# The last row tile of an attention and feed-forward kernel, computed and stored in three column pieces instead of two

## The chip, the cores and the metric

The kernel runs on one core of one Trainium2 chip. The metric is the device time of one execution in microseconds (us); a time is given as the median of several runs.

## What is computed

The reference has two parts. The first is a linear attention with a decay for each head, in blocks of 64 positions with a state that is carried from block to block. The second takes the attention's output as 3,072 rows of 512 and sends it through a feed-forward layer with a sine in it. Cut to what matters:

```python
# attention: q, k, v of (4, 8, 768, 64), lam of (8,)
for b in range(12):                                    # blocks of 64 positions
    intra = (qb @ kb^T * Dmask) @ vb                   # within the block
    inter = (qb * lam_pow) @ kv_state                  # from the blocks before
    out[block] = intra + inter
    kv_state = lam**64 * kv_state + (kb * rev_pow)^T @ vb

# feed-forward: x of (3072, 512), w_in of (512, 2048), w_out of (2048, 512)
h = x @ w_in
s = np.sin(alpha * h)
g = h + s * s / (alpha + 1e-09)
result = g @ w_out                                     # (3072, 512) float32
```

## The kernel before

The rows are treated in six groups of 512, each as four row tiles of 128. A long list, `ORDER`, gives the order in which every step is handed to its engine; a step is written `name.indices:engine:bank`, with T for TensorE, V for VectorE, A for ScalarE, G for GpSimd and S for SyncE. At its end stands group 5. The second product of a row tile is `f2` (sixteen matmuls into one bank of PSUM), its copy to SBUF is `oc`, and its store is `st`, once for each half of the partitions. The last row tile, the fourth of group 5, has steps of its own: `lt` for the matmuls and `ltc` for copy and store.

```python
# the end of ORDER
f2.5.1.0:T:2 f2.5.1.1:T f2.5.1.2:T f2.5.1.3:T f2.5.2.0:T:5 f2.5.2.1:T f2.5.2.2:T oc.5.1:V f2.5.2.3:T
st.5.1.0:S st.5.1.1:S lt.0:T:3 oc.5.2:V st.5.2.0:S lt.1:T:7 st.5.2.1:S ltc.0:A ltc.1:A
...
BANK = ("h0", "h1", "h2", "h3", "s0", "s1", "oa", "ob")

def psum(shape, dtype, name, bank):
    bank = bank[0] if isinstance(bank, list) else bank
    return ps.tile(shape, dtype, name=name, tag=BANK[bank], bufs=1)
...
outp = ctx.enter_context(tc.tile_pool(name="outp", bufs=4))
...
def copy(eng, out, in_):
    if eng is nc.scalar:
        nc.scalar.copy(out=out, in_=in_)                # line 281
    else:
        eng.tensor_copy(out=out, in_=in_)               # line 283
...
def ffn2(g, m, j, bank, **_):
    ...
        nc.tensor.matmul(out=ops[g, m][:], lhsT=gall[g][:, f, m * P:(m + 1) * P],   # line 524
                         rhs=w_out_sb[:, f, :], start=(f == 0), stop=(f == NFC - 1))

def store(g, m, par, **_):                              # line 539
    nc.sync.dma_start(out=out_rows(g, m)[par], in_=obs[g, m][par * D:(par + 1) * D, :])

last = {}

def last_tile(i, bank, **_):
    h = DM // 2                                         # 256 columns
    last[i] = psum([P, h], FP32, "ops", bank)
    for f in range(NFC):                                # 16 matmuls, line 547
        nc.tensor.matmul(out=last[i][:], lhsT=gall[NG - 1][:, f, 3 * P:],
                         rhs=w_out_sb[:, f, i * h:(i + 1) * h],
                         start=(f == 0), stop=(f == NFC - 1))

def last_copy(i, eng, **_):
    h = DM // 2
    rows = out_rows(NG - 1, 3)
    ob = outp.tile([P, h], FP32, name="ob")
    copy(eng, ob[:], last[i][:])
    for par, queue in ((0, nc.sync), (1, nc.scalar if i else nc.sync)):   # stores, line 557
        queue.dma_start(out=rows[par][:, i * h:(i + 1) * h], in_=ob[par * D:(par + 1) * D, :])
```

Two other steps have instructions of the form that the change brings in, 128 columns on the whole array or 128 columns from PSUM: `interm` (line 445), which multiplies the queries by the carried state, and `kv_copy`, which copies the key-value product (tile `kva`) out of PSUM with `copy`. Line 326 turns a 128 by 128 block with a matmul against the identity. Line 618 is the program's end, where all engines meet and SyncE waits for every store.

Of the kernel before, what the change touches and what calls it, by code (L numbers as in the profile page):

```python
# [11 lines left out]
FP32 = mybir.dt.float32  # L12
# [110 lines left out]
f2.4.2.3:T f2.4.3.0:T:0 f2.4.3.1:T f2.4.3.2:T f2.4.3.3:T f2.5.0.0:T:3 f2.5.0.1:T f2.5.0.2:T oc.4.2:V  # L123
oc.4.3:A st.4.3.0:S st.4.2.0:S st.4.3.1:S st.4.2.1:S f2.5.0.3:T oc.5.0:V st.5.0.0:S st.5.0.1:S
f2.5.1.0:T:2 f2.5.1.1:T f2.5.1.2:T f2.5.1.3:T f2.5.2.0:T:5 f2.5.2.1:T f2.5.2.2:T oc.5.1:V f2.5.2.3:T
st.5.1.0:S st.5.1.1:S lt.0:T:3 oc.5.2:V st.5.2.0:S lt.1:T:7 st.5.2.1:S ltc.0:A ltc.1:A
"""

@with_exitstack
def kernel(  # L130
# [12 lines left out]
    P = nc.NUM_PARTITIONS  # L143

    B, H, S, D = q.shape
# [5 lines left out]
    DM, DFF = moe_w_in.shape  # L151
# [17 lines left out]
    outp = ctx.enter_context(tc.tile_pool(name="outp", bufs=4))  # L169
# [29 lines left out]
    for c in range(2):  # L199
# [14 lines left out]
        out=mask[:], in0=it.rearrange("p two e -> p (two e)").unsqueeze(1)  # L214
# [20 lines left out]
    w_out_sb = wpool.tile([P, NFC, DM], BF16, name="w_out_sb")  # L235
# [5 lines left out]
# [3 lines that stand above are left out]
# [35 lines left out]
    def copy(eng, out, in_):  # L279
        if eng is nc.scalar:  # L280
            nc.scalar.copy(out=out, in_=in_)  # L281
        else:
            eng.tensor_copy(out=out, in_=in_)  # L283
# [193 lines left out]
    ops = {}  # L477
# [51 lines left out]
    def out_rows(g, m):  # L529
        _, tp, b, _, _ = where(4 * g + 2 * (m // 2))  # L530
        r0 = b * S + tp * W + (m % 2) * C
        return out[r0:r0 + C].rearrange("(p two) d -> two p d", two=2)
# [7 lines left out]

    last = {}

    def last_tile(i, bank, **_):
        h = DM // 2
        last[i] = psum([P, h], FP32, "ops", bank)
        for f in range(NFC):
            nc.tensor.matmul(out=last[i][:], lhsT=gall[NG - 1][:, f, 3 * P:],  # L547
                             rhs=w_out_sb[:, f, i * h:(i + 1) * h],
                             start=(f == 0), stop=(f == NFC - 1))

    def last_copy(i, eng, **_):
        h = DM // 2
        rows = out_rows(NG - 1, 3)
        ob = outp.tile([P, h], FP32, name="ob")
        copy(eng, ob[:], last[i][:])
        for par, queue in ((0, nc.sync), (1, nc.scalar if i else nc.sync)):
            queue.dma_start(out=rows[par][:, i * h:(i + 1) * h], in_=ob[par * D:(par + 1) * D, :])

    bz = ps.tile([P, 2 * P], FP32, name="bz", tag="h1", bufs=1)
    for _ in range(N0):  # L560
# [9 lines left out]
    def alphas(**_):  # L570
# [7 lines left out]
          "s": scores, "m": domask, "k": kvmm, "kc": kv_copy, "ap": alpha_turn, "al": alphas, "a": kv_decayed, "n": kv_next,  # L578
          "oi": interm, "o": outmm, "x": outev, "f1a": ffn1_first, "f1": ffn1, "sin": sine, "sqr": square,
          "stt": snake, "f2": ffn2, "oc": out_copy, "st": store, "lt": last_tile,  # L580
          "ltc": last_copy}
    def warm_up(n, tag):
# [40 lines left out]
```

## Time and profile before

| | before |
|---|---|
| time, median of 3 runs | 217.11 us (216.66 to 217.22) |
| span of the profiled run | 214.7 us |
| TensorE busy | 206.3 us, 96% of the span |
| last row tile: 32 matmuls of 128x256 | from 207.12 us, 3.66 us |
| copies of its two pieces on ScalarE | at 209.06 and 210.81 us, 0.37 us each |
| last two stores | issued at 211.21 us, one on SyncE and one on ScalarE |

Times inside a run count from the start of the profiled span. On the page, PE is TensorE's matmul side, PEld its weight loads, DVE VectorE, ACT ScalarE, POOL GpSimd and SP SyncE; a q behind an engine means its instruction queue, where the issue of a DMA is shown. A row of digits divides the span into 40 equal slices of 5.4 us, with the busy share of each in tenths. A group of instructions is given as line, engine, operation, the tiles written and read, the shapes, a count, the busy time and the mean length of one in ns; after the second bar stands how long the engine was idle before them and what ended that. A line of the timeline is start, length, engine, line, operation and count, with the idle time before it in brackets.

### The profile page before, as it was taken

The page shows a single profiled execution, that of the slowest core. Times are in us where ns is not written, and L with a number is a line of the kernel's source. Part 1 is how long each engine was busy: PE and PEld are TensorE (multiplying, and loading weights), DVE is VectorE, ACT ScalarE, POOL GpSimd, SP SyncE. Part 2 cuts the span into 40 slices and gives each one's busy share as a digit, 9 for nine tenths or more (in the row PEclk, how much of TensorE's full clock was granted, in tenths as well). Part 3 has the DMA queues.
Part 4 walks back from the last instruction along what each step waited for, and adds up shares of the span by engine and source line. Part 5 has one row for each costly group of instructions (what it writes and reads, how often), then busy time and mean ns, then how long its engine had stood idle before and what let it go on. Part 6 is the DMA issues. An engine that isn't in the chain of part 4 may idle for free.

```text
span 214.7 us, 5454 instructions
## 1 busy us (share of the span) xinstructions
PE 206.3 (96%) x2116; PEld 109.7 (51%) x2116; DVE 129.6 (60%) x234; ACT 123.8 (58%) x244; POOL 141.5 (66%) x208
## 2 busy tenths in 40 slices
PE   7999999897999999999998999999999999999992
PEld 5667544455744554455544554454454444444462
DVE  3894897157599854778756785726884635441120
ACT  2564993075899849996494496936635659131000
POOL 5496399699497999999998986709841738030000
PEclk9999999999999999999999999999999999999998
DMA  5999999999999999969799799720610000171624
GB/s 137 296 238 198 204 202 264 288 294 266 165 190 213 247 226 277 243 120 196 212 257 119 180 194 231 93 49 0 135 41 3 0 0 0 43 166 38 148 53 94
DMA packets 63849, 33.92 MB, mean 158 GB/s; under 512 B 19648, under 2 KB 60880, under 8 KB 63824
## 3 DMA queue, kind: packets, MB, share of 16 engines
q1 hardware_dynamic: 59488, 29.31, 62.6%
q0 software_dynamic: 4224, 4.19, 12.2%
q8 instruction: 16, 0.26, 0.6%
q10 hardware_dynamic: 112, 0.07, 0.1%
q14 instruction: 9, 0.07, 0.1%
HBM read 27.28 MB, written 6.29 MB: 156 GB/s over the span
## 4 chain that ended last, share of the span: by engine, by line
PE 72%; DMA 11%; POOL 4%; SPq 4%; ACT 4%; issue 2%; DVE 1%; POOLq 0%; ACTq 0%
PE ops L524 31%; PE hps L481 30%; DMA w_out_sb<-in_moe_w_out_dram 4%; SPq L258 4%; DMA st_v<-in_v_dram 3%; DMA QT<-KD 3%; PE sp L367 2%; PE okv L459 2%; ACT s L501 2%; DMA st_k<-in_k_dram 2%; PE ops L547 2%; PE okv L445 2%; POOL KD L299 1%; PE kvp L399 1%; POOL QL L299 1%
## 5 line engine op out<-in xcount | busy, mean ns | idle before, releaser
L481 PE MATMUL hps<-xt,w_in_sb 128*128 128x512 bf16 (+1 forms) x416 | 87.5, 363 | 0.0
L524 PE MATMUL ops<-w_out_sb,gall 128*128 128x512 bf16 x368 | 85.9, 379 | 0.6 <-DMA w_out_sb<-in_moe_w_out_dram 0.6
L515 DVE SCALAR_TENSOR_TENSOR gall<-s,r_sb,hps 128x512 bf16<-128x512 bf16 x96 | 68.3, 743 | 23.6 <-POOL s L510 12.0
L501 ACT ACTIVATE s<-hps,alpha_sb 128x512 bf16<-128x512 f32 x96 | 63.2, 689 | 25.8 <-PE hps L481 25.1
L510 POOL TENSOR_TENSOR s<-s 128x512 bf16<-128x512 bf16 x35 | 36.4, 1048 | 37.8 <-ACT s L501 37.1
L481 PEld LDWEIGHTS <-w_in_sb 128*128 128x128 bf16 x416 | 39.7, 98 | 40.7
L524 PEld LDWEIGHTS <-gall 128*128 128x128 bf16 x368 | 34.6, 98 | 40.2 <-issue 0.9
L377 DVE TENSOR_TENSOR ST<-sp,mask 128x512 bf16<-128x512 f32 x48 | 31.8, 684 | 4.4 <-PE sp L367 4.2
L508 ACT ACTIVATE s<-s 128x512 bf16<-128x512 bf16 x51 | 31.6, 633 | 1.0 <-DVE gall L515 0.4
L299 POOL TENSOR_TENSOR QL<-st_q,E 128x512 bf16<-128x512 f32 x23 | 24.0, 1045 | 3.7 <-DVE KD L299 2.1
L283 DVE COPY ob<-ops 128x512 f32<-128x512 f32 x12 | 8.3, 690 | 26.7 <-PE ops L524 23.4
L299 POOL TENSOR_TENSOR KD<-st_k,R 128x512 bf16<-128x512 f32 x22 | 22.9, 1045 | 2.0 <-DMA st_k<-in_k_dram 2.0
L424 POOL TENSOR_TENSOR kvbd<-kvx,LBD 128x256 bf16<-128x256 f32 x32 | 19.6, 614 | 2.5
L281 ACT COPY ob<-ops 128x512 f32<-128x512 f32 (+1 forms) x13 | 7.2, 555 | 23.3 <-PE ops L547 12.9
L281 ACT CAST xt<-okv 128x256 bf16<-128x256 f32 x29 | 9.8, 374 | 12.6 <-PE okv L459 12.4
L420 POOL TENSOR_TENSOR kvx<-kva,kvs 128x128 f32<-128x128 f32 x32 | 14.8, 463 | 1.4 <-ACT kva L281 1.2
L283 DVE CAST xt<-okv 128x256 bf16<-128x256 f32 x19 | 7.7, 419 | 11.0 <-PE okv L459 11.0
L281 ACT COPY kva<-kvp 128x128 f32<-128x128 f32 x26 | 6.4, 273 | 9.2 <-PE kvp L399 8.2
L281 ACT COPY QT<-pt 128x512 bf16<-128x512 bf16 x9 | 5.2, 585 | 10.1 <-PE pt L326 10.1
L367 PE MATMUL sp<-QT 64*64 64x128 bf16 x384 | 9.9, 219 | 0.9 <-DMA QT<-KD 0.9
L459 PE MATMUL okv<-ST,VB 64*64 64x128 bf16 x384 | 9.9, 220 | 0.0
L281 ACT CAST VB<-st_v 128x512 bf16<-128x512 f32 x14 | 8.6, 622 | 1.6 <-DMA st_v<-in_v_dram 1.6
(57 smaller groups left out, 126.9 us busy)
## 6 DMA issues: line engine op xcount, KB each, us to landing
st_q<-in_q_dram SPq DMA_DIRECT2D x24, 256.0 KB, 4.8
st_k<-in_k_dram SPq DMA_DIRECT2D x24, 256.0 KB, 4.7
st_v<-in_v_dram SPq DMA_DIRECT2D x24, 256.0 KB, 5.6
out_dram<-ob SPq DMA_DIRECT2D x46, 128.0 KB, 2.8
w_in_sb<-in_moe_w_in_dram POOLq DMA_DIRECT2D x4, 512.0 KB, 7.8
w_out_sb<-in_moe_w_out_dram POOLq DMA_DIRECT2D x4, 512.0 KB, 11.9
QT<-QL SPq DMA_TRANSPOSE x16, 3.2
QT<-KD SPq DMA_TRANSPOSE x16, 3.8
```

Of the source, the lines that this page charges most:

```text
L281: nc.scalar.copy(out=out, in_=in_)
L283: eng.tensor_copy(out=out, in_=in_)
L299: eng.tensor_tensor(out=t[:], in0=stage[u, j][:].rearrange("p h two e -> p two h e"), in1=tab[:, :, hh * HH:(hh + 1) * HH].unsqueeze(3).to ...
L377: nc.vector.tensor_tensor(out=stm[u][:, hd], in0=sps[u][hd][:], in1=mask[:].unsqueeze(2).to_broadcast([P, 2, 2, P]), op=ALU.mult)
L420: eng.tensor_tensor(out=t[:], in0=x, in1=prev[:], op=ALU.add)
L424: eng.tensor_tensor(out=kvbd[u, c][:], in0=x.unsqueeze(2).to_broadcast([P, 2, 2, D]), in1=LBD[:, 2 * hh:2 * hh + 2, :].unsqueeze(3).to_bro ...
L481: f1mm[g, f] = nc.tensor.matmul(out=hps[g, f][:].rearrange("p (b i) -> p b i", b=2)[:, bs] .rearrange("p b i -> p (b i)"), lhsT=w_in_sb[:, ...
L501: nc.scalar.activation(out=s1[g, f][:], in_=hps[g, f][:], func=ACTF.Sin, scale=alpha_sb[:, f:f + 1])
L508: nc.scalar.activation(out=s2[g, f][:], in_=x[:], func=ACTF.Square)
L510: eng.tensor_tensor(out=s2[g, f][:], in0=x[:], in1=x[:], op=ALU.mult)
L515: nc.vector.scalar_tensor_tensor(out=gall[g][:, f, :], in0=s2.pop((g, f))[:], scalar=r_sb[:, f:f + 1], in1=hps.pop((g, f))[:], op0=ALU.mul ...
L524: nc.tensor.matmul(out=ops[g, m][:], lhsT=gall[g][:, f, m * P:(m + 1) * P], rhs=w_out_sb[:, f, :], start=(f == 0), stop=(f == NFC - 1))
```

## The change

The last row tile is computed in three pieces of 256, 128 and 128 columns instead of two of 256. The first two are copied by ScalarE and the third by VectorE, so that the piece that ends last is smaller, and its copy is on an engine of its own. As before, the first piece is stored from SyncE's queue alone, and each later piece half from SyncE's and half from ScalarE's. The purpose is to shorten what is left to do once TensorE has finished. The number of multiplications and the bytes stored stay the same; there are 48 matmuls instead of 32 in this tile, three copies instead of two, and six stores instead of four.

```diff
-st.5.1.0:S st.5.1.1:S lt.0:T:3 oc.5.2:V st.5.2.0:S lt.1:T:7 st.5.2.1:S ltc.0:A ltc.1:A
+st.5.1.0:S st.5.1.1:S lt.0:T:3 oc.5.2:V st.5.2.0:S lt.1:T:7 st.5.2.1:S ltc.0:A lt.2:T:5 ltc.1:A
+ltc.2:V
...
+    LAST = ((0, 256), (256, 128), (384, 128))
+
     def last_tile(i, bank, **_):
-        h = DM // 2
-        last[i] = psum([P, h], FP32, "ops", bank)
+        c0, n = LAST[i]
+        last[i] = psum([P, n], FP32, "ops", bank)
         for f in range(NFC):
             nc.tensor.matmul(out=last[i][:], lhsT=gall[NG - 1][:, f, 3 * P:],
-                             rhs=w_out_sb[:, f, i * h:(i + 1) * h],
+                             rhs=w_out_sb[:, f, c0:c0 + n],
                              start=(f == 0), stop=(f == NFC - 1))
 
     def last_copy(i, eng, **_):
-        h = DM // 2
+        c0, n = LAST[i]
         rows = out_rows(NG - 1, 3)
-        ob = outp.tile([P, h], FP32, name="ob")
+        ob = outp.tile([P, n], FP32, name="ob")
         copy(eng, ob[:], last[i][:])
         for par, queue in ((0, nc.sync), (1, nc.scalar if i else nc.sync)):
-            queue.dma_start(out=rows[par][:, i * h:(i + 1) * h], in_=ob[par * D:(par + 1) * D, :])
+            queue.dma_start(out=rows[par][:, c0:c0 + n], in_=ob[par * D:(par + 1) * D, :])
```

## The prediction

> **What bounds the kernel now.** I read the page first, then the chain that ended last, then the timeline of the last five microseconds, because the change touches nothing earlier. From the page, busy times and TensorE's row of the slices:
>
> ```profile
> PE 206.3 (96%) x2116; PEld 109.7 (51%) x2116; DVE 129.6 (60%) x234; ACT 123.8 (58%) x244; POOL 141.5 (66%) x208
> ...
> PE   7999999897999999999998999999999999999992
> ```
>
> TensorE is busy nearly throughout, and only the last slice (5.4 us) falls to two tenths. The slack is therefore in that slice, and the chain of waits, asked for its last 20 us, says what fills it:
>
> ```profile
> 194.98 12.30 PE ops L524 x57
> 207.28 3.51 PE ops L547 x32
> 210.79 0.02 issue
> 210.81 0.37 ACT ob L281
> ```
>
> The columns are start, length and what it was. TensorE runs without a pause up to 210.79 us; line 547 is the last row tile, 32 matmuls in two pieces of 256 columns. ScalarE then copies the second piece and the chain stops at 211.18 us, but the span is 214.7 us. The 3.5 us left are the last two stores and the program's end. The timeline from 210.4 us on:
>
> ```profile
> 209.97 1.70 SPq L557 DMA_DIRECT2D out_dram<-ob  x2
> ...
> 210.81 0.37 ACT L281 COPY ob<-ops 128x256 f32<-128x256 f32 x1 [1.38 <-PE ops L547]
> 211.21 0.55 ACTq L557 DMA_DIRECT2D out_dram<-ob  x1
> ```
>
> and the DMA view of the window from 211.1 us, where the last column is the time from issue to landing:
>
> ```profile
> out_dram<-ob SPq DMA_DIRECT2D x1, 64.0 KB, 1.9
> out_dram<-ob ACTq DMA_DIRECT2D x1, 64.0 KB, 2.2
> ```
>
> The tail thus has four terms after the last matmul: copy 0.37, issue 0.03, landing 2.23 (211.21 to 213.44), and 1.23 from there to 214.67. In the trace's instructions the last term is SyncE's list of semaphore waits, one for each store semaphore, then the closing barrier. The wait for the store that lands last ends at 213.46; five more waits follow it at 0.06 us each, and the drain comes at 213.83.
>
> **What the Trainium skill says.** Its page "TensorE: Matmul & The Clock Gate", section "Wait — 56ns, not 53.3ns?", gives 55.6 ns from matmul to matmul at 128 columns on a warm clock; its section "Back-to-back issue gap" gives about 81 ns for a sustained stream in which every matmul has its own weight load. They disagree, and the changed pieces are such a stream, so the trace has to decide (next part). "DMA: Bandwidth & Descriptors", section "Anatomy of one DMA — SWDGE (gpsimd) path", puts about 2 us of a transfer down as fixed, mostly the receipt of the last write; the 1.9 to 2.5 us of the output stores here, though issued from other queues, fit that. The same page, "Issuing engines are not separate DMA queues", says that a second issuing engine saves only issue time. The trace agrees in kind: an issue occupies its queue for 0.47 to 0.60 us, and that alone is what the second queue takes off the path.
>
> **The change, part by part.** *Matmuls.* Piece 0 is as before: 16 matmuls of 256 columns, 0.109 us apart (3.66 us for 32, less the last one's 0.273, over 31 steps). The other 16 become 32 of 128 columns. The pace of that form, full array with a weight load for each, shows in line 445, in the timeline from 155.1 us:
>
> ```profile
> 155.18 0.39 PE L445 MATMUL okv<-QT,kvbd 128*128 128x128 bf16 x4
> ```
>
> A single one lasts 0.219 us, so (0.39 - 0.22) / 3 is 0.056 us a step, although one weight load lasts 0.098; the loads overlap. The longest such run in the trace is ten matmuls, where lines 326 and 445 follow each other near 50 us, and it keeps 0.056. So the two narrow pieces take 32 x 0.056 = 1.79 us where the wide one took 16 x 0.109 = 1.74: 0.05 later. But the last matmul itself is done 0.219 after its start instead of 0.273, which gives 0.05 back; counted from start to start (piece 1 begins at 208.86), piece 1 ends at 208.86 + 15 x 0.056 + 0.22 = 209.92 and piece 2 at 208.86 + 31 x 0.056 + 0.22 = 210.82, against 210.77 now. **+0.05.**
>
> *Copies.* Piece 2 goes through VectorE at 128 columns. The same form stands among the groups as the copy of the key-value product, on both engines:
>
> ```profile
> L281 ACT COPY kva<-kvp 128x128 f32<-128x128 f32 x26 | 6.4, 273 | 9.2 <-PE kvp L399 8.2 <-DVE kvbd L424 1.0
> ...
> L283 DVE COPY kva<-kvp 128x128 f32<-128x128 f32 x14 | 3.9, 283 | 1.8 <-PE kvp L399 1.7
> ```
>
> 0.283 instead of 0.372 is **-0.09**. With a start 0.04 after the matmul (as ScalarE's was, 0.036) the last copy runs from 210.86 to 211.14, where it now ends at 211.18. VectorE would have been as free as ScalarE: its last other copy ends at 208.06.
>
> *Issues.* SyncE's queue is busy with piece 0 until 210.57. Piece 1's copy is done at 209.96 + 0.27 = 210.23; ScalarE issues one half at 210.26 to 210.81, SyncE the other at about 210.63 to 211.10. Both are free again by 211.14, SyncE only just. So piece 2 is issued at about 211.19 on both queues against 211.21 now: **-0.02**, and not earlier. The work that goes before it hides completely.
>
> *Transfer.* The last two stores now have 64 rows of 512 bytes each instead of 1,024. In the trace a packet of 1,024 bytes on ScalarE's queue takes 69 ns in the median, one of 512 in the loads 27. Each of 16 engines carries 4 packets of a half, so up to 4 x 0.042 = 0.17 falls away; the packets don't all start together (the second half now spreads over 0.39 us), and I take **-0.13**. The rest of the 2.2 us has nothing to do with bytes. Piece 1's packets should move near 211.7 to 212.1, before those of piece 2 (from 212.3), so they don't collide.
>
> *Closing waits.* Two stores more move the last one two places on in the list of store semaphores, if they go on in rotation as the earlier stores do. Then three waits instead of five would follow it: 2 x 0.06 = 0.12. I am half sure of the order and take **-0.06**.
>
> Sum of what reaches the end, from the two times of issue: -0.02 - 0.13 - 0.06 = **-0.21 us**, and 217.11 - 0.21 = **216.9 us**. The copied columns and the stored bytes are unchanged in total; only the last piece is smaller, and the tail is made mostly of terms that don't shrink with it.
>
> **Rivals.** (a) *The weight load sets the pace.* If 32 narrow matmuls run at the Trainium skill's 81 ns and not at 56, piece 2 ends 31 x 0.025 = 0.78 us later, and the kernel gains nothing: about 217.7. Against it speaks the run of ten at 0.056; for it, that no run here is as long as 32. (b) *The landing is fixed.* If the transfer's size doesn't count at all and the list of waits doesn't help, only -0.02 is left: 217.1. For it speaks that stores of 128 KB land in 2.2 to 2.5 us and those of 64 KB in 1.9 to 2.2 us, a slope of 0.3 at most for 64 KB. (c) *SyncE's queue becomes the gate.* It has to take six issues in the tail less two on ScalarE, and it comes free at about 211.10. Should piece 1's issue take 0.60 instead of 0.47 and a wait instruction of 0.05 follow, piece 2's half starts at 211.3; but it has 0.3 us in hand, since SyncE's stores land in 1.9 and ScalarE's in 2.2. So this costs nothing in itself. (d) *ScalarE's queue wakes up.* Its one store before was its first since the start of the kernel and landed 0.3 later than SyncE's issued in the same moment. If that is a cost of first use, piece 1 pays it hidden, and the gain grows to 0.4 or 0.5: 216.6.
>
> **Range and chances.** All of this lies within 0.8 us, that is 0.4% of the time, while 2% is 4.3 us. The three runs before already differ by 0.56 us (216.66 to 217.22), more than my whole sum, so the range is mostly theirs: 216.4 to 217.5, with rival (d) near its lower and (a) just beyond its upper end. A result outside 2% would need something that is no part of the tail; I give each side one in a hundred.
>
> **What would show it right or wrong.** In the changed trace line 547's successor should show 48 matmuls, the narrow ones with a 0.056 step, and the last ending near 210.8; 0.08 means rival (a). The VectorE copy should last about 0.28 and end near 211.15; if it starts more than 0.1 after the last matmul, a wait has stepped in. ScalarE's last store should be issued near 211.2 and land in about 2.1 us; 2.2 means (b), 1.9 means (d). From that landing to the end it should be 1.1 to 1.2 us. The prediction is wrong if the start of line 547 moves away from 207.1 us, since nothing before it is changed, or if the last store waits for a semaphore of an earlier one.

## The result and the profile after

The changed kernel took 215.03 us in the median of 6 runs (214.49 to 215.63), the kernel before 216.54 us in the same two sets (216.18 to 217.22). The ratio is 0.9926, with a 95% interval from 0.9900 to 0.9951: 1.5 us less, within 2%, but below the predicted range of 216.4 to 217.5. The profiled run of the changed kernel spans 213.8 us. What follows shows that 0.34 us of this come from the change, that they come every time, and that the rest did not come again.

From the page of the changed kernel, the busy times and TensorE's row of the slices:

```profile
PE 204.0 (95%) x2104; PEld 110.1 (51%) x2132; DVE 129.8 (61%) x235; ACT 123.5 (58%) x244; POOL 141.4 (66%) x208
...
PE   7989999999999999999799999999999999999993
```

The picture is the old one; only the last slice moves, from two tenths to three. (Sixteen matmuls were added, and PEld counts 16 more; PE counts fewer because the trace misses some of its records.) The chain that ended last, over the last 20 us of the changed kernel, with start, length and what it was:

```profile
199.52 7.29 PE ops L525 x33
206.80 3.55 PE ops L550 x48
210.35 0.02 issue
210.38 0.29 DVE ob L284
```

Line 550 is the last row tile, now 48 matmuls, and VectorE's copy of 0.29 us stands where ScalarE's of 0.37 stood. The timeline of the changed kernel from 208.2 us shows the three copies and the stores behind them:

```profile
208.59 0.37 ACT L282 COPY ob<-ops 128x256 f32<-128x256 f32 x1 [11.52 <-PE ops L550]
208.99 2.38 SPq L560 DMA_DIRECT2D out_dram<-ob  x4
209.48 0.27 ACT L282 COPY ob<-ops 128x128 f32<-128x128 f32 x1 [0.52 <-PE ops L550]
209.78 1.39 ACTq L560 DMA_DIRECT2D out_dram<-ob  x2
210.38 0.29 DVE L284 COPY ob<-ops 128x128 f32<-128x128 f32 x1 [2.79 <-PE ops L550]
```

SyncE's queue has four stores in an unbroken row: 208.99 + 2.38 = 211.37. Its last one is issued at 210.83, while ScalarE's goes out at 210.70, 0.03 after the copy. To compare the tails, the windows view is cut into three stretches: the last row tile on TensorE, from its last matmul to the last landing, and from there to the end. The columns are the stretch, its length, the busy time of each engine with its instructions, the granted clock, and the DMA's share and rate. The kernel before:

```profile
207.12:210.78 3.66, 3.65 (x33) 3.03 (x31) 0.69 (x1) 0.37 (x1) 0.00 (x0) 1.00 0.37 83
210.78:213.45 2.67, 0.00 (x0) 0.00 (x0) 0.00 (x0) 0.37 (x1) 0.00 (x0) 0.96 0.36 83
213.45:214.67 1.22, 0.00 (x0) 0.00 (x0) 0.00 (x0) 0.00 (x0) 0.00 (x0) 0.50 0.00 0
```

and the changed kernel:

```profile
206.64:210.34 3.70, 3.70 (x49) 3.34 (x47) 0.69 (x1) 0.64 (x2) 0.00 (x0) 1.00 0.38 83
210.34:212.81 2.47, 0.00 (x0) 0.00 (x0) 0.29 (x1) 0.00 (x0) 0.00 (x0) 1.00 0.39 88
212.81:213.85 1.04, 0.00 (x0) 0.00 (x0) 0.00 (x0) 0.00 (x0) 0.00 (x0) 1.00 0.00 0
```

The length of each stretch is all that is needed: +0.04 on TensorE, -0.20 until the last landing, -0.18 until the end, in sum -0.34. The other 0.48 of the two profiles' difference lies ahead of the first stretch: the last row tile starts at 206.64 instead of 207.12, in a part of the program that the change does not touch. So two theories stood against each other. **TAIL**: the change gains 0.34 us in the tail, and the start of the tail merely scatters. **PROGRAM**: the longer instruction stream also moves what lies ahead of the tail, by about 1.1 us.

### The profile page after: what moved, and what is told of

Read it like the earlier page. It is cut to its first block, busy times and chain, and to the rows that moved or that the text cites. A ratio compares the mean times of both kernels' runs of the same rounds, so it can differ in the third digit from the quotient of the medians.

```text
span 213.8 us, 5465 instructions
## 1 busy us (share of the span) xinstructions
PE 204.0 (95%) x2104; PEld 110.1 (51%) x2132; DVE 129.8 (61%) x235; ACT 123.5 (58%) x244; POOL 141.4 (66%) x208
## 3 DMA queue, kind: packets, MB, share of 16 engines
q0 software_dynamic: 4224, 4.19, 12.4%
## 4 chain that ended last, share of the span: by engine, by line
PE 67%; POOL 12%; DMA 10%; issue 3%; ACT 2%; SPq 2%; DVE 2%; POOLq 0%; ACTq 0%
PE ops L525 27%; PE hps L482 24%; DMA w_out_sb<-in_moe_w_out_dram 4%; PE bz L564 3%; DMA QT<-KD 2%; PE okv L460 2%; POOL KD L300 2%; POOL kvbd L425 2%; PE sp L368 2%; PE bz L588 2%; DMA st_v<-in_v_dram 2%; POOL QL L300 2%; POOL kvx L421 2%; PE pt L327 2%; SPq L259 2%
## 5 line engine op out<-in xcount | busy, mean ns | idle before, releaser
L482 PE MATMUL hps<-xt,w_in_sb 128*128 128x512 bf16 (+1 forms) x404 | 86.4, 362 | 0.6 <-issue 0.2
L525 PE MATMUL ops<-w_out_sb,gall 128*128 128x512 bf16 x352 | 83.2, 379 | 2.1 <-issue 1.3
L284 DVE COPY ob<-ops 128x512 f32<-128x512 f32 (+1 forms) x13 | 8.6, 659 | 29.2 <-PE ops L525 23.6
L282 ACT COPY ob<-ops 128x512 f32<-128x512 f32 (+2 forms) x13 | 7.1, 547 | 22.4 <-PE ops L550 12.0
```

The costliest lines, as they stand in the source:

```text
L482: f1mm[g, f] = nc.tensor.matmul(out=hps[g, f][:].rearrange("p (b i) -> p b i", b=2)[:, bs] .rearrange("p b i -> p (b i)"), lhsT=w_in_sb[:, ...
```

## Experiments

All times of the tail below count from the start of the last row tile. Where no median is given, the kernel was run once, for its profile.

### The kernel before against itself, and the change again

No edit.

> The kernel before, unchanged, measured against itself. Both theories expect the same time within the scatter of the runs, a difference under 0.4 us. If it comes out 1 us or more away from itself, the measured gain of 1.5 us has a large part of chance in it. Its profile also gives a second look at the stages ahead of the last row tile (start of line 547 at 207.1 us in the first profile): theory TAIL (the change gains only behind the last row tile, 0.4 us by the profiles) expects that this start scatters by 0.5 us or more from run to run; theory PROGRAM (a longer instruction stream moves the earlier stages) expects it to stay within 0.2 us of 207.1.

> The changed kernel again. TAIL expects a gain of 0.4 to 0.5 us against the kernel before, and 7.2 us from the start of the last row tile to the end of the span. PROGRAM expects 1.3 to 1.7 us again, of which about 1.1 us lie ahead of the last row tile.

> The changed kernel unchanged once more, to see how its gain scatters from one set of runs to the next (1.5 us in the first, 0.2 to 0.5 in the second). Theory TAIL expects 0.3 to 0.4 us below the kernel before on average, each set off by up to 0.5, and 7.2 us from the start of the last row tile to the end. If the gain is 1.3 us or more again, then something ahead of the tail takes part, and TAIL falls.

The unchanged kernel took 216.55 us in the median of 22 runs, 0.9993 times the kernel before (0.9964 to 1.0022), but single runs lay between 214.75 and 218.55, and the 75 runs of the kernel before beside it between 214.91 and 218.88. The standard deviation is about 1 us, three times the gain in the tail. In the profile of this unchanged kernel the last row tile starts at 205.66 us, 1.46 before that of the first profile, and the tail is as long as it was: 7.54 us to the end. The prediction had taken a start away from 207.1 us as a sign of being wrong; the unchanged kernel moves it too.

The changed kernel took 216.19 us in 22 runs, 0.9977 of the kernel before (0.9952 to 1.0003), and in a third set, on another chip, 216.19 again, there 0.9993 (0.9968 to 1.0018). The means differ by 216.04 - 216.35 = -0.30 and 216.11 - 216.08 = +0.03 us; these means, like the ratios, leave out the few runs that lie over 1.5% above the fastest of their kernel. The 1.5 us did not come again. The tail did: 7.20 and 7.19 us in these two profiles, 7.21 in the first. The windows view of the second profile of the changed kernel:

```profile
206.75:210.45 3.70, 3.70 (x49) 3.34 (x47) 0.69 (x1) 0.64 (x2) 0.00 (x0) 1.00 0.37 83
210.45:212.92 2.47, 0.00 (x0) 0.00 (x0) 0.29 (x1) 0.00 (x0) 0.00 (x0) 1.00 0.39 88
212.92:213.95 1.03, 0.00 (x0) 0.00 (x0) 0.00 (x0) 0.00 (x0) 0.00 (x0) 1.00 0.00 0
```

The lengths agree with the first profile to 0.01 us. So a term of the tail can be read from one profile, while the whole time cannot show it in 22 runs.

### A longer instruction stream without the change

```diff
-... ltc.0:A ltc.1:A
+... ltc.0:A ltc.1:A w.16:T:h0
```

> The kernel before with 16 more matmuls on zeros of 256 columns (1.7 us of TensorE) behind its last row tile, into a bank that nobody reads. TensorE's stream is as long as that of the changed kernel (32 instructions more), but they run beside the last stores: done near 212.6 us, before the last landing at 213.4. TAIL expects the time of the kernel before, within 0.3 us. PROGRAM expects most of the 1.1 us that don't come from the tail, so 215.4 to 215.8 where the kernel before takes 216.5.

216.02 us in the median, 1.0000 of the kernel before (0.9971 to 1.0029). A gain of 1.1 us would be 0.995 and is outside. The tail is 7.55 us, as before, with the added matmuls beside the stores. PROGRAM falls, as far as the length of TensorE's stream is what it means.

### The second copy on VectorE, with two pieces

```diff
-... ltc.0:A ltc.1:A
+... ltc.0:A ltc.1:V
```

> The kernel before with one part of the change alone: two pieces of 256 columns as they were, the second copied by VectorE instead of ScalarE. TAIL expects no gain: VectorE needs about 0.42 us for 256 columns where ScalarE needs 0.37, and the last store is issued 0.05 us later, so the time of the kernel before within 0.3 us. PROGRAM expects the same, since the streams keep their length.

0.9981 of the kernel before (0.9958 to 1.0004), no clear difference. The copy of 256 columns ends at 4.12 instead of 4.07, the stores go out at 4.15 instead of 4.09, and the tail is 7.58 us. (This profile is of the slowest of the 22 runs, 218.71 us; its last row tile starts at 209.33, and the tail alone is compared.) By itself the other engine costs 0.04 to 0.05, as expected.

### First piece from two queues, in the changed kernel and in the kernel before

The same edit in both:

```diff
-        for par, queue in ((0, nc.sync), (1, nc.scalar if i else nc.sync)):
+        for par, queue in ((0, nc.sync), (1, nc.scalar)):
```

> The changed kernel with the first piece stored from two queues as well (second half on ScalarE). All times from the start of the last row tile. In the changed kernel SyncE's queue is free for piece 2 only at 4.19, 0.13 after ScalarE's store (4.06), and SyncE's store lands last at 6.17; end 7.21. Theory GATE (SyncE's queue is behind with its issues, and only that delays the last landing) expects both last stores issued at 4.06, the last landing at 6.0 to 6.05 and the end at 7.05 to 7.1. Theory PAIR (of two stores issued at the same moment the second one is served after the first and lands 0.3 later) expects one of them to land at 6.25 to 6.35 and the end at 7.3: then the staggering of the changed kernel was worth more than the delay cost.

> The kernel before with the first piece's second half stored from ScalarE's queue, so that ScalarE's last store is no longer its first since the start. Before, ScalarE's last store took 2.23 from issue to landing and SyncE's, issued in the same moment, 1.94. Theory FIRST (a queue's first store in a long while is slower) expects ScalarE's to land after 1.95 too, the last landing at 6.04 and the end at 7.25. Theory PAIR (the second of two simultaneous stores is served after the first) expects 2.23 again, 6.33 and 7.54. The issue of the first piece on ScalarE ends at 2.9, before its next copy at 3.69, and delays nothing in either theory.

In the changed kernel with this edit the two last stores did go out together, at 4.05 and 4.06. SyncE's landed at 5.93, ScalarE's at 6.21, later than the last landing of the changed kernel (6.17). The DMA view of its last window, with the size of each store and its time from issue to landing:

```profile
out_dram<-ob SPq DMA_DIRECT2D x1, 32.0 KB, 1.9
out_dram<-ob ACTq DMA_DIRECT2D x1, 32.0 KB, 2.2
```

and that of the kernel before with the edit:

```profile
out_dram<-ob SPq DMA_DIRECT2D x1, 64.0 KB, 2.0
out_dram<-ob ACTq DMA_DIRECT2D x1, 64.0 KB, 2.2
```

In the second, ScalarE's last store is not its first, and still takes 2.22 us: FIRST falls. In both, the store from ScalarE's queue that is issued in the same moment as SyncE's lands about 0.3 later. GATE falls, and PAIR's 0.3 holds (the landing at 6.21 is 0.04 earlier than it expected, the end is as expected): delaying SyncE's store by 0.13 in the changed kernel costs nothing, since the second store would have landed at that time anyway. PAIR's wording, that the second is served after the first, does not hold.

In the packets of the trace of the kernel before, SyncE's last store runs from 5.21 to 5.67 and ScalarE's from 5.50 to 5.94: the two overlap, and only the start of the second is 0.29 later. It is 0.29 in the changed kernel with the edit too (5.23 and 5.52), and 0.28 in the changed kernel (5.19 and 5.47), where the issues are 0.13 apart. From issue to landing half the bytes seem to change little, 2.22 to 2.16 and SyncE's 1.97 to 1.88. But with 512 bytes a row the packets began 0.04 to 0.05 later after the issue here; from the first packet to the landing it is 0.80 and 0.84 with 1,024 bytes, 0.70 and 0.71 with 512.

The rows of the windows view for the changed kernel with the edit (the middle one):

```profile
209.64:212.16 2.52, 0.00 (x1) 0.00 (x0) 0.29 (x1) 0.00 (x0) 0.00 (x0) 1.00 0.38 86
212.16:213.26 1.10, 0.00 (x0) 0.00 (x0) 0.00 (x0) 0.00 (x0) 0.00 (x0) 1.00 0.00 0
```

2.52 instead of 2.47, and the last landing is now ScalarE's, which stands one place earlier in the list of closing waits: 1.10 instead of 1.04. The tail is 7.32 us, 0.11 longer. In the kernel before the edit left the tail at 7.54.

### More stores early, so that the last ones stand last in the list

In the kernel before with two row tiles split, in the changed kernel with one (`(4, 2)` alone):

```diff
-        nc.sync.dma_start(out=out_rows(g, m)[par], in_=obs[g, m][par * D:(par + 1) * D, :])
+        parts = 2 if (g, m) in ((4, 2), (4, 3)) else 1
+        n = D // parts
+        for r in range(0, D, n):
+            nc.sync.dma_start(out=out_rows(g, m)[par][r:r + n],
+                              in_=obs[g, m][par * D + r:par * D + r + n, :])
```

> The kernel before with four stores more, ten microseconds and more ahead of the last row tile: the stores of two row tiles of the group before are split into two each, same bytes. The last stores stay as they were, but their semaphores move four places on in the list of closing waits, ScalarE's from the 4th of 9 to the 8th. Theory LIST (the waits behind the one that ends last cost 0.06 us each) expects the last landing unchanged at 6.33 and 0.98 from there to the end instead of 1.22: end at 7.31 instead of 7.54. Its rival, a fixed closing time, expects 1.22 and 7.54.

> The changed kernel with two stores more, well ahead of the last row tile: the two stores of one row tile of the group before are split into two each, same bytes. The semaphores of the two stores that end last move two places on in the list of closing waits, to its last two places. Theory LIST expects the last landing unchanged at 6.17 after the start of the last row tile, 0.92 from there to the end instead of 1.04, and the end at 7.09 instead of 7.21. In the time that is 0.1 us below the changed kernel and 0.45 below the kernel before, both smaller than the scatter of single runs. A fixed closing time expects 7.21.

The kernel before with four stores more, last two stretches of its tail:

```profile
211.06:213.70 2.64, 0.00 (x0) 0.00 (x0) 0.00 (x0) 0.37 (x1) 0.00 (x0) 0.95 0.37 85
213.70:214.69 0.99, 0.00 (x0) 0.00 (x0) 0.00 (x0) 0.00 (x0) 0.00 (x0) 0.50 0.00 0
```

The changed kernel with two more:

```profile
209.40:211.88 2.48, 0.00 (x1) 0.00 (x0) 0.29 (x1) 0.00 (x0) 0.00 (x0) 1.00 0.39 88
211.88:212.81 0.93, 0.00 (x0) 0.00 (x0) 0.00 (x0) 0.00 (x0) 0.00 (x0) 1.00 0.00 0
```

The stretch to the last landing nearly stays (2.64 after 2.67, 2.48 after 2.47), and the closing time falls from 1.22 to 0.99 and from 1.04 to 0.93. LIST holds. (The split stores are issued 6 to 10 us before the last row tile starts, not ten and more.) The tail of the second kernel is 7.10 us, the shortest of all, 0.44 below the kernel before. Its time, 215.93 us against 215.95 (1.0002, from 0.9978 to 1.0026), does not show it; 0.44 us is 0.2%, inside that interval.

### Third piece on ScalarE

```diff
-ltc.2:V
+ltc.2:A
```

> The changed kernel with its third piece copied by ScalarE as well. If VectorE's copy is worth nothing here (ScalarE has issued its store of piece 1 by 3.68, before the last matmul is done at 3.70), the copy starts at 3.73 to 3.76 and ends at 4.00 to 4.03, SyncE's store still goes out at 4.19, and the end stays at 7.2. If ScalarE's own issue holds its copy up, the copy ends after 4.1 and the end comes 0.1 later.

The timeline of this kernel:

```profile
209.10 0.55 ACTq L560 DMA_DIRECT2D out_dram<-ob  x1
209.84 0.27 ACT L282 COPY ob<-ops 128x128 f32<-128x128 f32 x1 [0.77 <-PE ops L550]
```

ScalarE had issued its store by 209.10 + 0.55 = 209.65, and the last matmul was done at 209.66; yet the copy began at 209.84. It ends at 4.14 instead of 4.03, and the tail is 7.35 us, 0.14 longer. So VectorE's part in the change is worth 0.14 us, and not because its copy is quicker (0.29 against 0.27). What stands between the issue and the copy in ScalarE's queue shows in the view of line 282 from 209.6 us:

```profile
L282 ACTq EVENT_SEMAPHORE  x2: 38/38/38, 209.7 to 209.8; - x2
```

These are the copy's own waits, on semaphores of earlier stores and of VectorE that had all been signalled 0.6 us or more before. They start 0.04 after the issue's end and follow each other, with the copy behind them, at 0.077: 0.04 + 2 x 0.077 = 0.19, which is the whole delay. In the changed kernel with its first piece on two queues, the second copy comes 0.27 after ScalarE's issue, and three stand there (the same view from 208.8 us): 0.04 + 3 x 0.077 = 0.27.

```profile
L282 ACTq EVENT_SEMAPHORE  x3: 38/38/38, 208.9 to 209.0; - x3
```

In the changed kernel itself the same three lie at 1.95 to 2.15, while TensorE still works, and hold up nothing. No run took these waits away, so the sum is what speaks for them.

This kernel also tells queue from order. ScalarE's store went out first here, at 4.17, and SyncE's at 4.19, as late as in the changed kernel; SyncE's landed last, at 6.30 against 6.02. So it is the later of the two stores that lands 0.3 later, and not ScalarE's. The packets start at 5.32 and 5.61, again 0.28 apart: with ScalarE's store 0.11 later than in the changed kernel, the one behind it comes later too, and that is the 0.14.

### Two pieces of 384 and 128 columns

```diff
+    LAST = ((0, 384), (384, 128))
```

with the slices of the change, and the second piece copied by VectorE.

> The kernel before with two pieces of 384 and 128 columns, the second copied by VectorE: the small last piece of the change without its third piece. Piece 0 is done at about 2.8 and its copy at 3.3 (512 columns take ScalarE 0.59, 256 take 0.37), SyncE's two stores of it go out at 3.3 and 3.85 and hold the queue until 4.4; the last matmul is done at 3.7 and VectorE's copy at 4.03. If the queue counts (SyncE's store of piece 1 goes out at 4.45), that store lands at 6.35 and the end is at 7.5, as in the kernel before: three pieces are needed to keep the queue free. If only the bytes of the last piece counted, the last landing would be at 6.2 and the end at 7.35.

The tail is 7.70 us, longer than that of the kernel before and than both expectations. SyncE's queue was still issuing the large piece; its store of the small one went out at 4.51, as expected if the queue counts, but took 2.03 us to land, at 6.54 instead of 6.35. So the small last piece gains nothing here, with the larger piece holding the queue ahead of it. Whether the larger piece's bytes lengthen the landing was not tried.

### Taking the waits for the transposes away

In both kernels:

```diff
-        qkt[u] = work.tile([P, 2, 2, 2, P], BF16, name="QT", bufs=NQT)
+        qkt[u] = work.tile([P, 2, 2, 2, P], BF16, name="QT7" if u == 7 else "QT",
+                           bufs=1 if u == 7 else NQT - 1)
+        used[u] = qkt[min(u, 7)]
 ...
-        QT = qkt[u]
+        QT = used[u]
```

From unit 8 on the products read unit 7's turned tile instead of their own, so their values are other than the reference's; nothing waits for the later transposes.

> The kernel before without its waits for the transposes by DMA: from unit 8 on, the scores and the product with the state read the turned queries and keys of unit 7 instead of their own (the output isn't the reference's). All transposes still run, into their buffers, with nobody waiting for them; unit 7's tile has a buffer of its own and the others share three instead of four. In eleven profiles so far TensorE waited between 0 and 3.0 us for them, and the start of the last row tile lay between 205.7 and 209.3. Theory WAITS (these waits are the main part of the scatter) expects no wait for the transposes in the profile, a median 0.8 to 1.2 us below the kernel before, and a standard deviation of the runs of 0.5 us or less where the kernel before has 0.8 to 1.0. If the scatter comes from the earlier waits (loads and weights in the first 55 us, 0.8 to 2.3 us in the profiles), the standard deviation stays at 0.8 or more.

> The changed kernel with the same waits taken away in the same way. Against the same edit of the kernel before, TAIL expects 0.34 us less, and 7.2 against 7.54 us from the start of the last row tile to the end. If WAITS holds too, the scatter is small enough for the medians to show it: a difference of 0.2 to 0.5. A difference of 1 us or more would mean that the change acts ahead of the tail after all.

The reason to try this: in the third profile of the changed kernel, TensorE's waits between 55 us and the tail are these alone (engine and line, what for, then the total, the times and the longest one):

```profile
PE sp L368 <- DMA QT<-KD: 1.4, 2, 0.9
```

and in the second profile of the kernel before, whose tail began 1.3 us earlier, there are none. Without them the kernel before took 215.80 us, 0.9972 of the kernel before as it was (0.9950 to 0.9994), and the changed one 215.27, 0.9944 of the same (0.9924 to 0.9963). The edit is worth 0.8 us in the median. But the standard deviations stayed at 0.76 and 0.82 us where the kernel before has 0.80: WAITS falls as the main cause of the scatter. The same view of the kernel before without them shows other waits in their place:

```profile
PE hps L484 <- DVE gall L518: 1.4, 1, 1.4
PE okv L448 <- POOL kvbd L427: 0.7, 1, 0.7
```

What lies behind these, the loads or something else, was not tried and stays open. Between the two edited kernels the means differ by 215.36 - 215.90 = -0.54 us, with an interval of 0.48 to each side by the scatter of the 22 runs of each, and the tails are 7.21 and 7.54.

## Why the prediction was wrong

**Range and chances.** This step failed, and the predicted time with it. It took the 0.56 us between three runs for the kernel's scatter and their median, 217.11, for its time; from that came 216.4 to 217.5, where 215.03 was measured. The 75 later runs of the unchanged kernel spread over 4 us, with a median of 216.37. Three runs drawn from them at random lie within 0.56 us in about 8 of 100 draws (an estimate from these runs). The tail does not mend it: with the measured -0.34 in place of -0.21 the prediction would have been 216.8.

The 1.5 us of the first two sets did not come again. Three later comparisons with 22 runs of the changed kernel each, the third with the last edit above in both kernels, gave -0.30, +0.03 and -0.54 us, on average -0.27 with 0.25 to each side. That agrees with the predicted -0.21 and with the -0.34 of the profiles, and not with -1.5. Why the first two sets lay so far apart stays open. A longer TensorE stream does not do it, and the tail is always the same. Scatter of single runs is a weak explanation: six runs drawn at random from each of the two large sets (75 runs of the kernel before, 22 of the changed one) differ by 1.5 us in this direction in one or two of 100 draws (an estimate from these runs), and the runs of the first two sets lay closer together (standard deviations of 0.45 and 0.41 us) than those of the later ones (0.8 to 1.2). Whether something common to a whole set moved it was not tried.

**Matmuls.** Right. Predicted 0.05 later at 0.056 us a step; the last matmul ends at 3.70 instead of 3.66, and the narrow ones start 0.056 apart. The weight loads do not set the pace over 32 narrow matmuls, so rival (a) is out, and the 81 ns that the Trainium skill gives in "TensorE: Matmul & The Clock Gate", section "Back-to-back issue gap", are not what this stream shows.

**Copies.** Right: 0.29 instead of 0.37, ending at 4.03 instead of 4.07.

**Issues.** Wrong for SyncE's store, without consequence for the last landing. Both were to go out 0.02 earlier; ScalarE's did (4.06 instead of 4.09), but SyncE's went out at 4.19: its issue of piece 1 began at 3.55 and lasted 0.54, and a semaphore instruction at 4.14 followed. Rival (c) had named this moment, and that it costs nothing in itself, but the reason that it gave was not the one: SyncE's stores do not land sooner than ScalarE's, the later of the two lands 0.3 later, and it does so even when it is issued 0.13 later. That this came out even was luck.

**Transfer.** Right. Issue and transfer together were to bring the last landing forward by 0.15; it came 0.16 earlier, at 6.17 instead of 6.33. The -0.13 from the bytes shows from the first packet to the landing: 0.83 for the last store before, 0.70 after. The first of the two stores goes out 0.03 earlier, and the second's packets start 0.29 and 0.28 after the first's: that is the rest. What the prediction quotes of a transfer's fixed 2 us, that they are mostly the receipt of the last write, does not show in this trace: of the 2.23 us before, 1.41 passed ahead of the first packet, 0.44 with the packets and 0.39 after them.

**Closing waits.** This is the term of the tail that was mis-sized. Its mechanism was right, its size a third: I took half of 0.12, that is -0.06; it was -0.18. The last two stores moved two places on as assumed, but SyncE's instead of ScalarE's is now the last to land, and it stands one place further on: two waits follow it instead of five. The waits from the one that ends last on, in the kernel before and in the changed one:

```profile
L618 SPq EVENT_SEMAPHORE  x6: 27/28/28, 213.5 to 213.8; - x6
```

```profile
L621 SPq EVENT_SEMAPHORE  x3: 28/28/28, 212.8 to 212.9; - x3
```

Of the 0.12 that the term lacked, 0.06 had been left out for doubt about the order; the other 0.06 is SyncE's late issue, which the prediction had not carried over to the list. In the changed kernel with its first piece on two queues, ScalarE's store lands last again, and the closing time is 1.10 instead of 1.04.

**Rivals.** (b), a fixed landing, is out: the bytes gave 0.13 and the list of closing waits 0.18. (d), a slow first use of ScalarE's queue, is out: its later stores are as slow when they are the second of a pair. The sign given for (d), a landing after 1.9 us, did come (ScalarE's last store took 1.83 in the second and third profile of the changed kernel), but because it was the first of the two.

## What to carry to other kernels

Find out how far single runs of the unchanged kernel scatter before a gain of under one per cent is believed; compare the changed stretch in profiles instead, where its length may agree to 0.01 us while the start of it wanders by more than a microsecond. At the end of a program, count issues per queue, and don't expect two stores issued in the same moment to land together. Look for the waits ahead of a last copy in its engine's queue: if the engine comes to them late, they cost time although nothing is left to wait for, and an engine that has passed them before is the better one.

## What was not expected of the hardware

- Of two stores of 64 rows each, issued 0.005 to 0.02 us apart from SyncE and ScalarE, the later one landed 0.24 to 0.31 us after the other, with 1,024 bytes a row (6.03 and 6.33) as with 512 (5.93 and 6.21), and also when SyncE's was the later one (6.02 and 6.30). Issued 0.13 apart, ScalarE's first, they still landed 0.28 apart (5.89 and 6.17).
- A semaphore instruction in ScalarE's queue cost 0.077 us although nothing was left to wait for, by the sum over two kernels: a copy began 0.20 us after its own store issue had ended with two of them in between (3.68 and 3.88), and 0.27 with three (2.90 and 3.17).
- The order in which the program's end waits for its stores counts: each wait behind the one that ends last cost 0.06 us, and four stores added more than ten microseconds before the last ones took 0.23 us off the closing time of the kernel before.
